# Loads of float64 weight pieces moved ahead of stores, kvb filled by two masked copies, wo1 spread over more steps

## The chip, the cores and the metric

The kernel runs on one core of a Trainium2 chip. The metric is the device time of one execution in microseconds (us). A core has TensorE (matmul; PE, and PEld for the load of its stationary operand), VectorE (DVE), ScalarE (ACT), GpSimd (POOL) and SyncE (SP); in this kernel every DMA is issued from SP's queue.

## The reference

Three layers, one after the other. An attention with 32 learned memory slots, over 8 batches, 8 heads, 576 positions, head size 64:

```python
a = phi - np.max(phi, axis=2, keepdims=True)
a = np.exp(a)
a = a / (np.sum(a, axis=2, keepdims=True) + 1e-09)
k_m = np.einsum('bhsm,bhsd->bhmd', a, k)
v_m = np.einsum('bhsm,bhsd->bhmd', a, v)
scores = scale * np.matmul(q, k_m.transpose(0, 1, 3, 2))
...
return np.matmul(attn, v_m)          # attn = softmax(scores)
```

Its output, as 4608 tokens of 512, goes through `h = max(max(x @ w1, x @ w2), x @ w3)` with 768 columns and `h @ w_out`, and that result through `(sigmoid(x @ w_gate) * (x @ w_val)) @ w_out` with 1536 columns. The activations are float32; the seven weight matrices are float64 and are turned into float32 on the chip.

## The kernel before

Matmuls take their operands as two parts, a rounded one and the rest, and add three products (`PASSES`).

**Weights.** A float64 weight comes as pieces of 128x384 64-bit words. `w_fetch` loads one into a tile `raw` (three buffers); `w_f32` (L122 to L126) makes float32 of it with two ScalarE and three VectorE instructions, the last of which (L126) reads `raw` for the last time; `w_split` makes the two parts on ScalarE (L131) and another engine (L73). `w_want` puts the next piece on the list `wq`, `w_have` takes the oldest from it, converts it, and for the first pass stores the split piece to `wxs`, from where later passes read it. `w_step` does a `w_have` and then the next `w_want`; `w_fill` fills `wq` up to three. `wx` (24 pieces) and `wo1` (8 pieces) go this way. The 48 pieces `wb` of the last layer go through `b_want` and `b_step`: convert the oldest, store it to `wbf`, load the next; `b_start` loads two ahead.

**Attention.** A group n is four heads of one batch; there are 16. `a0` takes the softmax of phi, with the reciprocal sums in `rs`; `a1` transposes it; `a2` multiplies it with k and v (L207) and copies the result, scaled by `rs`, into `kvb`: head s has partitions 32s to 32s+31, and goes into half `s % 2` of the columns, the other half staying at zero, so that the transposes of L227 in `a3` give block matrices. `kvb` is one of two tiles, filled with zeros once at the start. `a4` and `a5` make the second softmax.

**The passes.** The first part of the kernel is four passes of two batches each, `p`, of NS + NX = 24 + 16 steps `s`: `g_step` (v_m times wx, L342), `h_step` (the first layer, L369), then from step 24 on `x2_step` (times wo1, L392), one block d of 128 output columns in four steps. Block d reads pieces 2d and 2d+1 of wo1. Attention groups of the next pass are spread over the steps. `at(pos, fn)` hangs a weight step behind step `int(pos)`. The last layer follows (L687, L754).

**Order.** The instructions of an engine don't run in the program's order: the tile framework plans each engine's order in a timeline of its own, takes what is ready there, and prefers what stands earlier in the program. A load can go as soon as its tile's buffer is free. Two things bind the SP queue further: until `queue["in order"] = False`, every DMA stays in program order; and in the first pass `later` keeps the loads of phi, kv and q behind the last weight load traced so far.

Of the kernel before, what the change touches and what calls it, by code (L numbers as in the profile page):

```python
# [8 lines left out]
F32 = mybir.dt.float32  # L9
# [3 lines left out]
AF = mybir.ActivationFunctionType  # L13
ALU = mybir.AluOpType
AX = mybir.AxisListType
# [3 lines left out]
def attn_moe_kernel(  # L19
# [28 lines left out]
    vec, act, pool, pe, sync = nc.vector, nc.scalar, nc.gpsimd, nc.tensor, nc.sync  # L48
# [3 lines left out]
    def dma(o, i):  # L52
        ins = sync.dma_start(o, i)
        if queue["in order"]:
            tc.keep_in_program_order(ins)
        return ins
# [6 lines left out]
    def f32(ap):  # L63
        return ap.bitcast(F32)
# [16 lines left out]
    const = ctx.enter_context(tc.tile_pool(name="const", bufs=1))  # L81
    ident = const.tile([128, 128], F32, name="ident")
# [5 lines left out]
    att = tc.alloc_tile_pool(name="att", bufs=1, side="right")  # L88
    psA = tc.alloc_tile_pool(name="psA", bufs=8, space=PSUM)

    def bank():
        return psA.tile([128, 512], F32, tag="ps", name="ps")
# [12 lines left out]
    def w_fetch(pl, src):  # L105
        if not is64:
            w = pl.tile([128, PC], F32, tag="wf", name="wf", bufs=3)
            queue["last weights"] = dma(w, src)
            return w
        raw = pl.tile([128, PC], I64, tag="raw", name="raw", bufs=3)  # L110
        queue["last weights"] = dma(raw, src)
        return raw
# [17 lines left out]
    def w_split(w, hi, lo, eng=None):  # L130
        act.copy(hi, w)  # L131
        sub(eng or pool, lo, w, f32(hi))
# [35 lines left out]
        A[n]["q"].append(t)  # L168


    KVB = []
    for i in range(2):
        t = att.tile([128, 2, 2, 64], F32, name=f"kvb{i}")
        pool.memset(t, 0.0)
        KVB.append(t)

    def a0(n):
        st = A[n]
        nm = att.tile([128, 1], F32, tag="nm", name="nm", bufs=4)
        vec.tensor_reduce(out=nm, in_=st["phi"], axis=AX.X, op=ALU.max, negate=True)  # L180
        ss = att.tile([128, 1], F32, tag="ss", name="ss", bufs=4)
        et = st["et"] = att.tile([128, S], F32, tag="et", name="et", bufs=2)
        act.activation(out=et, in_=st["phi"], func=AF.Exp, bias=nm, accum_out=ss)
        rs = st["rs"] = att.tile([128, 1], F32, tag="rs", name="rs", bufs=4)
        vec.tensor_scalar(out=rs, in0=ss, scalar1=EPS, scalar2=None, op0=ALU.add)
        vec.reciprocal(out=rs, in_=rs)
        yield

    def a1(n):
# [10 lines left out]
    def a2(n):  # L200
        st = A[n]
        p = bank()
        es = st["es"]
        for c in range(5):
            r = 128 if c < 4 else 64
            for s in range(4):
                pe.matmul(  # L207
                    p[32 * s:32 * s + 32, :128],
                    lhsT=es[:r, c, 32 * s:32 * s + 32],
                    rhs=st["kv"][c][:r, 128 * s:128 * s + 128],  # L210
                    start=(c == 0), stop=(c == 4),
                )
        yield
        kvb = st["kvb"] = KVB[n % 2]
        for s in range(4):
            r = slice(32 * s, 32 * s + 32)
            act.activation(out=kvb[r, :, s % 2], in_=p[r, :128].rearrange("p (x d) -> p x d", x=2),
                           func=AF.Copy, scale=st["rs"][r])

    VT = {}  # L220

# [69 lines left out]
    wq = []  # L291

    def w_want(j, hp, p):
        if p == 0:
            wq.append((j, hp, p, w_fetch(mid, wx[j, hp] if j >= 0 else wo1[hp])))
        else:
            t = mid.tile([128, 2, PC], F32R, tag="wx", name="wx", bufs=6)
            dma(f32(t), wxs[j, hp])
            wq.append((j, hp, p, t))

    def w_have():
        j, hp, p, w = wq.pop(0)
        if j < 0:
            w = w_f32(mid, w)
            r = slice(hp * PC, hp * PC + PC)
            w_split(w, wo1_t[:, 0, r], wo1_t[:, 1, r])
            return
        if p == 0:
            w = w_f32(mid, w)
            t = mid.tile([128, 2, PC], F32R, tag="wx", name="wx", bufs=6)  # L310
            w_split(w, t[:, 0], t[:, 1])
            dma(wxs[j, hp], f32(t))
            w = t
        WX[j, hp] = w
# [4 lines left out]
    def b_want():  # L319
        if bplan:  # L320
            i, n = bplan.pop(0)
            bq.append((i, n, w_fetch(mid, wb[i, n])))

    def b_step():
        if not bq:
            return
        i, n, w = bq.pop(0)
        dma(wbf[i, :, n * PC:n * PC + PC], w_f32(mid, w))
        b_want()

    G = {}
    PASSES = ((1, 0), (0, 1), (0, 0))
# [201 lines left out]
    plan = []  # L534

    def w_step():
        if not wq:
            return
        w_have()
        if plan:  # L540
            w_want(*plan.pop(0))

    def w_fill():
        while plan and len(wq) < 3:
            w_want(*plan.pop(0))

    for t in range(len(stages) + 5):
# [37 lines left out]
    for p in range(NP):  # L585
        last = p == NP - 1
        side = {}

        def at(pos, fn, *a):
            side.setdefault(min(int(pos), NS + NX - 1), []).append((fn, a))  # L590

        if last:
            att.release()
            br = tc.alloc_tile_pool(name="br", bufs=1, side="right", reuse_waits="tile")
            at(NS, x_load, 0)
            at(NS, tw_load, 0)
            at(NS + 1, x_sums, 0, 0)
            at(NS + 2, x_sums, 0, 1)
            at(NS + 2, t_make, 0, ORDER[0])
            for n, pr in enumerate(ORDER):  # L600
                at(NS + 3 + n * 0.8, x_split, 0, pr, vec if n % 2 else None)
                if n:
                    at(NS + 8 + n * 0.8, t_make, 0, pr)
            at(NS + 14, wo_make, 0)
        for j in range(2, J):
            for hp in range(4):
                at(4 * (j - 2) + hp, w_step)
        if p == 0:
            def wo1_begin():
                plan.extend((-1, n, 0) for n in range(J * DM // PC))  # L610
                w_fill()
            at(4 * (J - 2) - 3, wo1_begin)
            for n in range(J * DM // PC):
                at(22 + n / 2, w_step)
        if not last:
            def w1_begin(p=p):
                plan.extend((j, hp, p + 1) for j in range(J) for hp in range(4))
                w_fill()
            at(29, w1_begin)
            for n in range(8):  # L620
                at(30 + n, w_step)
        if p == 0:
            for k in (0, 2, 4):
                at(3 + k // 2, later, load_ahead, k, 3)
        if p:
            n_b = 22 if last else 13
            end = NS - 1 if last else NS + NX
            at(0, b_start)
            for n in range(n_b):
                at(n * end / n_b, b_step)  # L630
        a_at, a_st = (0, 1.3) if p else (10, 1.1)
        atts = {}
        if not last:
            q = [(k, n) for n in range(4 * p + 4, 4 * p + 8) for k in range(len(stages))]
            for i, x in enumerate(q):
                atts.setdefault(min(int(a_at + i * a_st), NS + NX - 1), []).append(x)
            for n in range(4 * p + 4, 4 * p + 8):
                at(max(NS, a_at + a_st * (6 * (n - 4 * p) - 18)), a_split, n)
        for s in range(NS + NX):
            if last and s == NS:  # L640
                mid.release()
                b1 = tc.alloc_tile_pool(name="b1", bufs=1, side="right", reuse_waits="tile")
            gens = []
            for k, n in atts.get(s, ()):
                if len(atts[s]) > 1:
                    run(stages[k](n))
                    load_ahead(k, n)
                else:
                    gens.append(stages[k](n))
            if s < NS:  # L650
                j, u = divmod(s, 4)
                if j + 1 < J:
                    gens.append(g_step(p, j + 1, u))
                gens.append(h_step(p, j, u))
            else:
                d, u = divmod(s - NS, 4)
                if not last and 32 <= s < 36:
                    gens.append(g_step(p + 1, 0, s - 32))
                gens.append(x2_step(p, u, d))
            run(*gens)  # L660
            if len(atts.get(s, ())) == 1:
                if p == 0:
                    later(load_ahead, *atts[s][0])
                else:
                    load_ahead(*atts[s][0])
            for fn, a in side.get(s, ()):
                fn(*a)
# [201 lines left out]
```

## Time and profile before

| | us |
|---|---|
| median of 3 runs | 1414.42 |
| lowest and highest of them | 1409.95, 1415.02 |
| the profiled execution, its own time | 1413.25 |
| its span in the trace | 1411.5 |

| engine | busy us | share of the span |
|---|---|---|
| PE | 1353.1 | 96% |
| PEld | 1191.1 | 84% |
| DVE | 875.0 | 62% |
| ACT | 583.3 | 41% |
| POOL | 517.7 | 37% |

The time of an execution is that of the run; the span is what the trace covers of it, and lies 1.75 us below. Busy shares are means over stages that differ. A wait is listed with the engine that waits, the line, and what released it. A matmul's duration overlaps with its neighbours', so a number of matmuls in a stretch says more than their single durations.

### The profile page before, as it was taken

How to read it: one execution, taken by the hardware profiler on the slowest of the kernel's cores; microseconds unless marked ns; L12 is line 12 of the kernel's file. 1: busy time of each engine (PE TensorE's matmuls, PEld its weight loads, DVE VectorE, ACT ScalarE, POOL GpSimd, SP SyncE). 2: the span in 40 equal slices, each digit the busy share in tenths (PEclk: the TensorE clock that was granted, in tenths of full speed). 3: DMA queues.
4: the chain of work that ended last, by engine and by line, in shares of the span. 5: the costliest groups of instructions: out<-in, count | busy, mean ns of one | idle time of the engine just before them, and what ended most of it. 6: DMA issues, size and time to landing. Idle time of an engine off the chain costs nothing.

```text
span 1411.5 us, 22167 instructions
## 1 busy us (share of the span) xinstructions
PE 1353.1 (96%) x7864; PEld 1191.1 (84%) x7864; DVE 875.0 (62%) x1532; ACT 583.3 (41%) x1236; POOL 517.7 (37%) x456
## 2 busy tenths in 40 slices
PE   6588899989999999999999999999999999999998
PEld 3478798879999999878888888888888899999997
DVE  5989989987773575667765344454454534554454
ACT  6768667754653353353333221232222322133221
POOL 2666422241233126554487111371112712161211
PEclk8779999999999999999999999999999999999999
DMA  9588799878552433775546554465454666566651
GB/s 316 192 260 278 257 328 321 291 249 276 185 162 92 159 95 119 281 265 213 204 175 228 167 179 161 160 198 194 149 168 175 209 219 229 188 230 225 223 202 67
DMA packets 112269, 292.43 MB, mean 207 GB/s; under 512 B 12576, under 2 KB 28960, under 8 KB 112160
## 3 DMA queue, kind: packets, MB, share of 16 engines
q1 hardware_dynamic: 112160, 291.03, 60.8%
q8 instruction: 62, 1.02, 0.3%
q14 instruction: 47, 0.39, 0.1%
HBM read 224.92 MB, written 66.06 MB: 206 GB/s over the span
## 4 chain that ended last, share of the span: by engine, by line
PE 80%; DVE 7%; DMA 5%; issue 3%; ACT 3%; POOL 1%; SPq 0%; DVEq 0%; POOLq 0%; ACTq 0%
PE po L754 21%; PE px L687 15%; PE ps L369 11%; PE pz L687 10%; PE pv L687 10%; PE ps L392 8%; PE ps L342 3%; DMA raw<-wb_dram 1%; DVE ca L124 1%; DVE g L73 1%; PE ps L245 1%; DVE ca L126 1%; ACT g L356 1%; PE ps L207 1%; DMA q<-qT_dram 1%
## 5 line engine op out<-in xcount | busy, mean ns | idle before, releaser
L754 PE MATMUL po<-wo,gg 128*128 128x512 f32 x1296 | 332.8, 395 | 1.0 <-POOL gg L73 1.0
L73 POOL TENSOR_TENSOR gg<-gf,gg 128x512 fp32r<-128x512 f32 (+1 forms) x120 | 143.5, 1196 | 478.1 <-ACT gg L720 478.1
L754 PEld LDWEIGHTS po<-wo,gg 128*128 128x128 f32 x1296 | 242.5, 188 | 55.2 <-POOL gg L73 1.5
L369 PE MATMUL ps<-attn,g 128*128 128x288 f32 x1728 | 258.3, 304 | 18.3 <-POOL s L73 5.6
L369 PEld LDWEIGHTS ps<-attn,g 128*128 128x128 f32 x1728 | 247.5, 195 | 26.1 <-POOL s L73 5.9
L687 PE MATMUL px<-xa,tb 128*128 128x512 f32 (+1 forms) x1080 | 245.3, 369 | 1.6 <-ACT sg L710 1.3
L766 DVE TENSOR_TENSOR acc<-po,acc 128x512 f32<-128x512 f32 x180 | 124.3, 691 | 182.7 <-PE po L754 182.2
L687 PEld LDWEIGHTS px<-xa,tb 128*128 128x128 f32 x1080 | 198.1, 188 | 31.6 <-POOL tb L73 1.7
L687 PE MATMUL pz<-xa,tb 128*128 128x512 f32 (+1 forms) x720 | 171.0, 370 | 0.4 <-DVE x L70 0.4
L687 PE MATMUL pv<-xa,tb 128*128 128x512 f32 (+1 forms) x720 | 170.6, 369 | 0.0
L392 PE MATMUL ps<-h,wo 128*128 128x288 f32 x1152 | 161.4, 299 | 0.0
L392 PEld LDWEIGHTS ps<-h,wo 128*128 128x128 f32 x1152 | 157.3, 192 | 2.2 <-issue 1.9
L73 POOL TENSOR_TENSOR h<-hm,h 128x288 fp32r<-128x288 f32 x96 | 82.9, 865 | 196.7 <-ACT h L68 102.8
L687 PEld LDWEIGHTS pz<-xa,tb 128*128 128x128 f32 x720 | 132.2, 188 | 20.7 <-DVE x L70 0.8
L687 PEld LDWEIGHTS pv<-xa,tb 128*128 128x128 f32 x720 | 131.8, 188 | 18.9
L720 ACT CAST gg<-gf 128x512 fp32r<-128x512 f32 (+1 forms) x120 | 69.4, 579 | 179.6 <-DVE gf L716 132.7
L738 DVE TENSOR_TENSOR u<-pz,p 128x512 f32<-128x512 f32 (+1 forms) x120 | 76.2, 635 | 95.3 <-PE pz L687 89.2
L73 DVE TENSOR_TENSOR g<-ps,g 64x384 fp32r<-64x384 f32 x180 | 99.3, 552 | 32.7 <-ACT g L356 29.3
L356 ACT CAST g<-ps 64x384 fp32r<-64x384 f32 x192 | 90.7, 474 | 56.4 <-PE ps L342 30.4
L710 ACT ACTIVATE sg<-sg 128x512 f32<-128x512 f32 (+1 forms) x90 | 53.1, 590 | 146.8 <-DVE sg L708 146.6
L73 POOL TENSOR_TENSOR xa<-xf,xa 128x512 fp32r<-128x512 f32 (+1 forms) x64 | 78.7, 1252 | 19.9 <-ACT xa L131 19.9
L342 PE MATMUL ps<-wx,vt 128*128 128x384 f32 x288 | 73.0, 365 | 7.3 <-DVE g L73 3.0
(91 smaller groups left out, 1415.6 us busy)
## 6 DMA issues: line engine op xcount, KB each, us to landing
tb<-tbs SPq DMA_DIRECT2D x168, 512.0 KB, 3.7
wx<-wxs SPq DMA_DIRECT2D x72, 384.0 KB, 4.1
wo<-wos SPq DMA_DIRECT2D x48, 512.0 KB, 5.1
tbs<-tb SPq DMA_DIRECT2D x42, 512.0 KB, 2.9
raw<-wb_dram SPq DMA_DIRECT2D x48, 384.0 KB, 4.8
kv<-kvm_dram SPq DMA_DIRECT2D x48, 256.0 KB, 5.2
raw<-wx_dram SPq DMA_DIRECT2D x24, 384.0 KB, 4.0
wxs<-wx SPq DMA_DIRECT2D x24, 384.0 KB, 5.0
```

Source lines behind the costliest of these rows:

```text
L73: eng.tensor_tensor(out=o, in0=a, in1=b, op=ALU.subtract)
L124: vec.tensor_scalar(out=ai, in0=ai, scalar1=3, scalar2=None, op0=ALU.logical_shift_left)
L342: pe.matmul(ps[:, :384], lhsT=vt[:, x, 2 * e:2 * e + 2].rearrange("p a m -> p (a m)"), rhs=w[:, y], start=(n == 0), stop=(n == 2),)
L356: act.copy(t[r, 0], ps[r, :384])
L369: pe.matmul(ps[w][:, :U], lhsT=G[b, j, g][:, x, 128 * w:128 * w + 128], rhs=at[:, y, hf * U:hf * U + U], start=(n == 0), stop=(n == 5),)
L392: pe.matmul(ps[:, :U], lhsT=wo1_t[:, x, (d * J + j) * 128:(d * J + j) * 128 + 128], rhs=H[u, j][:, y], start=(n == 0), stop=(n == 3 * J - 1),)
L687: pe.matmul(ps[:, :half], lhsT=w[:, a, o:o + 128], rhs=x[:, k, c, :half], start=(first and n == 0), stop=(n == 5), skip_group_check=not first,
L710: act.activation(out=sg, in_=src, func=AF.Sigmoid)
L720: act.copy(t[:, 0, :half], gf)
L738: vec.tensor_tensor(out=u, in0=ps[:, :half], in1=E["p1", v], op=ALU.add)
L754: pe.matmul(ps, lhsT=GG[sc, j, c, h][:, x, 128 * m:128 * m + 128], rhs=WO[sc, j, h][:, y], start=(n == 0), stop=(n == 5),)
L766: vec.tensor_tensor(out=t, in0=ps, in1=t, op=ALU.add)
```

## The change

`b_step` and `w_step` issue the load of the next piece before they take, convert and store the piece in hand; `w_fill` fills to two. `kvb` becomes a tile that is written whole for each group: two copies over all 128 partitions, one for each half of the columns, with a scale `rm` that is `rs` where the head belongs to that half and zero elsewhere. `rm` is the product of `rs` and `mask`, which is summed once from the identity matrix. The eight steps of wo1, before behind the steps 22, 22, 23, 23, 24, 24, 25, 25, stand behind 22, 22, 24, 25, 27, 28, 29, 29.

```diff
@@ -168,11 +168,8 @@
         A[n]["q"].append(t)
 
 
-    KVB = []
-    for i in range(2):
-        t = att.tile([128, 2, 2, 64], F32, name=f"kvb{i}")
-        pool.memset(t, 0.0)
-        KVB.append(t)
+    mask = const.tile([128, 2], F32, name="mask")
+    vec.tensor_reduce(out=mask, in_=ident.rearrange("p (a s m) -> p s a m", s=2, m=32), axis=AX.XY, op=ALU.add)
 
     def a0(n):
         st = A[n]
@@ -184,6 +181,8 @@
         rs = st["rs"] = att.tile([128, 1], F32, tag="rs", name="rs", bufs=4)
         vec.tensor_scalar(out=rs, in0=ss, scalar1=EPS, scalar2=None, op0=ALU.add)
         vec.reciprocal(out=rs, in_=rs)
+        rm = st["rm"] = att.tile([128, 2], F32, tag="rm", name="rm", bufs=4)
+        vec.tensor_scalar(out=rm, in0=mask, scalar1=rs, scalar2=None, op0=ALU.mult)
         yield
 
     def a1(n):
@@ -211,11 +210,10 @@
                     start=(c == 0), stop=(c == 4),
                 )
         yield
-        kvb = st["kvb"] = KVB[n % 2]
-        for s in range(4):
-            r = slice(32 * s, 32 * s + 32)
-            act.activation(out=kvb[r, :, s % 2], in_=p[r, :128].rearrange("p (x d) -> p x d", x=2),
-                           func=AF.Copy, scale=st["rs"][r])
+        kvb = st["kvb"] = att.tile([128, 2, 2, 64], F32, tag="kvb", name="kvb", bufs=2)
+        for e in range(2):
+            act.activation(out=kvb[:, :, e], in_=p[:, :128].rearrange("p (x d) -> p x d", x=2),
+                           func=AF.Copy, scale=st["rm"][:, e:e + 1])
 
     VT = {}
 
@@ -324,9 +322,9 @@
     def b_step():
         if not bq:
             return
+        b_want()
         i, n, w = bq.pop(0)
         dma(wbf[i, :, n * PC:n * PC + PC], w_f32(mid, w))
-        b_want()
 
     G = {}
     PASSES = ((1, 0), (0, 1), (0, 0))
@@ -536,12 +534,12 @@
     def w_step():
         if not wq:
             return
-        w_have()
         if plan:
             w_want(*plan.pop(0))
+        w_have()
 
     def w_fill():
-        while plan and len(wq) < 3:
+        while plan and len(wq) < 2:
             w_want(*plan.pop(0))
 
     for t in range(len(stages) + 5):
@@ -611,7 +609,7 @@
                 w_fill()
             at(4 * (J - 2) - 3, wo1_begin)
             for n in range(J * DM // PC):
-                at(22 + n / 2, w_step)
+                at((22, 22, 24, 25, 27, 28, 29, 29)[n], w_step)
         if not last:
             def w1_begin(p=p):
                 plan.extend((j, hp, p + 1) for j in range(J) for hp in range(4))
```

## Rows read from the trace of the kernel before

**Rows 1.** Busy us (and instructions) of each engine in two stretches, clock, DMA.
```profile
48.00:350.00 302.00, 268.95 (x2023) 249.69 (x2023) 273.10 (x555) 203.03 (x476) 123.63 (x113) 0.92 0.82 278
...
583.00:1411.00 828.00, 822.05 (x3798) 699.36 (x3798) 427.32 (x636) 242.11 (x436) 288.02 (x238) 1.00 0.56 194
```

**Rows 2.** What matmuls waited for, 48 to 350 us: total, times, longest.
```profile
PE ps L227 <- ACT kvb L217: 8.3, 3, 5.5
```

**Rows 3.** Timeline, 306 to 318 us: start, us, engine, what [idle before].
```profile
306.42 0.53 DVE L126 SCALAR_TENSOR_TENSOR ca<-raw,ca 128x384 uint32<-128x384 uint32 x1
...
306.98 0.33 SPq L53 DMA_DIRECT2D wbf<-ca  x1
...
307.40 0.38 SPq L53 DMA_DIRECT2D raw<-wb_dram  x1
...
311.10 0.55 ACT L122 ACTIVATE ca<-raw 128x384 f32<-128x384 f32 x1 [1.59 <-DMA raw<-wb_dram]
...
311.99 1.46 ACT L217 ACTIVATE kvb<-ps,rs 32x128 f32<-32x128 f32 x4
...
313.50 0.69 PE L227 MATMUL ps<-ident,kvb 128*128 128x128 f32 x2 [5.52 <-ACT kvb L217]
...
313.84 4.09 PE L392 MATMUL ps<-h,wo 128*128 128x288 f32 x18
```

**Rows 4.** Timeline, 167 to 174 us.
```profile
167.05 0.55 ACT L122 ACTIVATE ca<-raw 128x384 f32<-128x384 f32 x1 [1.17 <-DMA raw<-wb_dram]
...
169.45 0.44 PE L227 MATMUL ps<-ident,kvb 128*128 128x128 f32 x2 [2.26 <-ACT kvb L217]
...
169.64 4.10 PE L392 MATMUL ps<-h,wo 128*128 128x288 f32 x18
```

**Rows 5.** Chain that ended last, in order of time: start, us, what.
```profile
319.06 9.72 PE ps L392 x72
```

**Rows 6.** What ScalarE waited for, 150 to 350 us: total, times, longest.
```profile
ACT ca L122 <- DMA raw<-wb_dram: 23.6, 22, 3.0
```

**Rows 7.** The DMA queue (SP) in order of time, 148 to 159 us.
```profile
148.52 0.33 SPq L53 DMA_DIRECT2D raw<-wb_dram  x1
...
153.41 0.33 SPq L53 DMA_DIRECT2D raw<-wb_dram  x1
```

**Rows 8.** The same queue, 158 to 194 us.
```profile
158.58 0.33 SPq L53 DMA_DIRECT2D raw<-wb_dram  x1
162.86 0.33 SPq L53 DMA_DIRECT2D wbf<-ca  x1
...
192.38 1.44 SPq L53 DMA_DIRECT2D wbf<-ca  x2
193.88 0.50 SPq L53 DMA_DIRECT2D raw<-wb_dram  x1
```

**Rows 9.** Groups by line and shape, whole run: busy us, mean ns | idle before.
```profile
L217 ACT ACTIVATE kvb<-ps,rs 32x128 f32<-32x128 f32 x64 | 23.0, 359 | 4.6 <-PE ps L207 3.7
...
L271 DVE TENSOR_SCALAR sm<-sm 128x18 f32<-128x18 f32 x16 | 5.2, 324 | 0.1
...
L230 ACT COPY kt<-ps 128x128 f32<-128x128 f32 x16 | 4.2, 264 | 2.9 <-PE ps L227 2.8
...
L185 DVE TENSOR_SCALAR rs<-ss 128x1 f32<-128x1 f32 x16 | 2.3, 141 | 4.3 <-ACT et L183 4.3
```

**Rows 10.** Timeline, first 5 us: first work of VectorE.
```profile
3.71 0.75 DVE L180 TENSOR_REDUCE nm<-phi 128x1 f32<-128x576 f32 x1 [3.71 <-DMA phi<-phiT_dram]
```

**Rows 11.** The DMA queue (SP), first pass, 83 to 85 us.
```profile
83.90 0.38 SPq L53 DMA_DIRECT2D raw<-wx_dram  x1
84.33 0.45 SPq L53 DMA_DIRECT2D phi<-phiT_dram  x1
```

**Rows 12.** Work on tile wo, 100 to 240 us: ns min/median/max, first and last start.
```profile
L392 PE MATMUL ps<-h,wo x288: 290/295/442, 160.0 to 211.6; 128*128 128x288 f32 x144
L131 ACT CAST wo<-ca x8: 512/512/515, 122.3 to 158.5; 128x384 fp32r<-128x384 f32 x8
```

## The prediction

> **What bounds the kernel now.** I read the busy time by stretches first, since the share over the whole span mixes stages. In the second half TensorE is busy 822 of 828 us at the full clock of 2.4 GHz [rows 1]; nothing that this change touches runs there, and nothing is to be had there. From 48 to 350 us it is another picture: TensorE is busy 269 of 302 us, at a granted clock of 0.92, while VectorE is busy 273 us and ScalarE 203 us. So about 33 us of idle TensorE, and the time at the lower level of 1.2 GHz that follows idle stretches, are all that a change in the front can win. The conversion of the float64 weights fills VectorE's gaps in it.
>
> Next, the list of waits of the matmul queue in this stretch: the largest entry is the transposes of L227, which wait 8.3 us in three stops for the copies to kvb in L217 [rows 2]. The timeline shows what the two large ones are made of. At 308 us TensorE stands 5.52 us before L227, because ScalarE has a conversion of L122 ahead of L217 in its queue and waits 1.59 us for that one's raw piece, until 311.10 us; then come the four copies, 1.46 us [rows 3]. At 167 us it is the same picture, smaller: 1.17 us for a raw piece, then the copies, 2.26 us of idle TensorE [rows 4]. After each, a group of 18 matmuls of L392 takes 4.09 or 4.10 us [rows 3, 4], where 72 of them take 9.72 us later, 2.43 us for 18 [rows 5]: the clock fell behind the stop, for another 1.67 us each time. In all ScalarE waits 23.6 us, 22 times, for raw pieces of wb between 150 and 350 us [rows 6]; most of it stops no matmul.
>
> **The change, part by part.** First, the load ahead of the store. In the program, b_step issues the store of piece n, then the load of piece n+2; afterwards the load comes first. If the SP queue followed the program, the load would have stood behind a store that waits for the conversion. But the queue of before shows three loads of wb, at 148.52, 153.41 [rows 7] and 158.58 us, ahead of the first store at 162.86 us [rows 8]. The planner already takes the third load ahead. What holds a load is its buffer: the last conversion step of an older piece ends at 306.42 + 0.53 = 306.95 us, its store goes at 306.98 and the load into the freed buffer at 307.40 us [rows 3]. That store is three pieces older than the load, so it is ahead of it in both programs. I went through the 48 loads of wb so: 36 go within 1.5 us after their buffer is free. Only where two stores go together, as at 192.38 us with the load at 193.88 [rows 8], can the new order help, by about one store's 0.3 to 1.4 us of issue. Cost and gain: 0, with a bound of 23.6 us of ScalarE's waits from above [rows 6] if the loads do come earlier, and of 1.5 us of SP issue from below.
>
> For w_step the same holds more plainly: with two filled instead of three and the load first in each step, the loads and stores come in the same sequence as before (L2, S0, L3, S1, ...), with the same three buffers. Only the place in the program moves by a step. That place matters in one spot: loads of phi, kv and q in the first pass are queued behind the last weight load traced so far, as phi at 84.33 us right behind the weight piece at 83.90 [rows 11]. They may now go one weight piece, some 4 us, sooner. The list of [rows 2] has no wait for a DMA in it, so I count 0; if they delay a weight piece, it is by their own issue, 0.45 us for one.
>
> Second, the copies. Four ScalarE copies of 32 partitions become two of 128. The elements in a partition stay 128, and a copy of 128 by 128 without scale takes 264 ns where one of 32 by 128 with a scale takes 359 ns [rows 9]: the time is not set by the partitions. I take 359 ns each (bounds 264 and, if nothing is saved by halving their number, 2 x 359). A group of heads saves 2 x 0.36 = 0.72 us on ScalarE, 16 groups 11.5 us, 8 groups in the stretch 5.7 us. On the path it counts where L227 waits: in the two large stops 0.72 us each, in the small third one (8.3 - 5.52 - 2.26 = 0.5 us) 0.5 us: together 1.9 us. Elsewhere ScalarE's shorter queue is covered by VectorE's.
>
> What it adds: 16 products rm of 128x2 on VectorE. The rows around are 141 ns for 128x1 and 324 ns for 128x18 [rows 9]; 128x2 is nearer to the first, so 0.14 us. Eight in the stretch make 1.1 us (2.6 us at 324 ns; 0 where VectorE is idle, and it is busy 90% of the stretch [rows 1]): I count 1.0 us. Its place in the queue is ahead of the other groups' reductions, and the copies now wait for rm, 0.14 us behind rs, two stages before they are due. The mask is one reduction of 128x128 at the start, under the 0.75 us that a reduction of 128x576 takes, and VectorE does nothing until 3.71 us, when phi lands [rows 10]; it costs 0 there, and up to 0.75 us if that cover were gone. Two fills of kvb on GpSimd go, ahead of anything that waits.
>
> Third, wo1. Its eight pieces were cast between 122.3 and 158.5 us, the first matmul that reads them starts at 160.0 us and the last of the pass at 211.6 us [rows 12]. They run as fast as buffers come free, long before the steps that the program names, so a later step changes only who goes first among ready work. The second pair of pieces is needed only after the first four groups of 18 matmuls. I count 0; the gain is bounded by the two stops, the loss is the last rival below.
>
> Sum: 1413.25 - 1.9 + 1.0 = 1412.35, say 1412 us. The profiled execution's 1413.25 us stands 1.2 us under the median of the three runs shown, 1414.42. A measurement of this kernel tells about 0.5% from no change, so below 1407.3 is faster and above 1421.5 slower.
>
> **The rivals.** *The stops go.* If the new sequence (loads that do come earlier, or merely another order of ScalarE's queue) takes L217 out from behind waiting conversions, both stops vanish with their clocks: 5.52 + 2.26 + 2 x 1.67 = 11.1 us, 1402 us. For it: both have the one form, and the change shortens or moves two of its three parts. Against: the loads are held by buffers, which the change leaves at three.
>
> *VectorE sets the pace.* It is the fullest engine beside TensorE in the stretch. Then ScalarE's saving is worth nothing and the 16 products cost their whole time, 1.1 to 2.6 us in the stretch: 1415 us, no measurable change either. The Trainium skill says as much (Perfetto Trace Analysis, Identifying the Most-Contended Engine): improve the engine with the highest occupancy first. By that rule the halved copies give nothing, and the trace speaks against it. By the rows alone: VectorE still has 29 us idle in the stretch [rows 1], and TensorE stops 8.3 us for ScalarE's copies [rows 2], so this case gets the smallest chance.
>
> *wo1 comes late.* If the planner does follow the later steps, x2_step of the first pass reaches its second block before pieces 2 and 3 are split, and TensorE stops. Pieces were cast every (158.5 - 122.3) / 7 = 5.2 us [rows 12]; two that are still out cost 10.4 us, and the clock behind the stop 1.67 us: 1425 us. It decides from the second missing piece; one alone gives 1420. Against it: every piece was cast before the first of them was read.
>
> **How the numbers follow.** Forecast, 1412 us: 0.38. VectorE's pace, 1415 us: 0.10. The stops go, 1402 us: 0.33. wo1 late, 1425 us: 0.19. So faster 0.33, the same 0.48, slower 0.19. The forecast's own range is 1409 to 1418: 1.9 us of saving or none, 2.6 us of rm, and the runs' spread of 2.5 us to either side. The range given goes 4 us below the rival at 1402, an eighth of the 33 us of idle TensorE that a new order could take along, to 1398, and up to a single late piece, 1420; two late pieces, 0.19, lie outside.
>
> **What would show it.** Right: the group of L217 with 32 instead of 64 at about 0.36 us; loads of raw still within 1 us after a conversion ends; three loads of wb ahead of the first store; the 583 to 1411 us part unchanged; TensorE idle about 32 us in the front. Wrong: stops before L227 gone or longer than 5 us, a shorter list of ScalarE's waits for raw, matmuls of L392 that wait for wo1, or casts of wo1 after 160 us. Since each engine's order is planned anew, the weakest step is that the two stops stay where they are.

## The result, and the profile after

The changed kernel takes 1394.26 us (median of four runs, 1389.95 to 1395.26) against 1414.29 us for the kernel before: ratio 0.9859, interval 0.9830 to 0.9888. It is 20 us faster. The forecast was 1412 us, and the time lies below the range of 1398 to 1420. The profiled execution took 1393.47 us, with a span of 1391.6 us.

The first look is again at the busy time by stretches, here of the kernel after, for the stretches of [rows 1] (the last one ends 20 us sooner):

```profile
48.00:350.00 302.00, 274.58 (x2128) 254.15 (x2129) 277.45 (x578) 200.47 (x475) 125.83 (x115) 0.95 0.84 280
...
583.00:1391.00 808.00, 803.94 (x3766) 692.74 (x3764) 419.68 (x628) 238.53 (x432) 285.30 (x236) 1.00 0.58 196
```

The front gets 105 more matmuls done in the same 302 us (2128 for 2023). The surprise is the second row. In [rows 1] 3798 matmuls took 822.05 us of busy time, 216.4 ns each; now 3766 take 803.94 us, 213.5 ns each, at the same full clock and with no instruction of that part changed. Two windows of 100 us inside the last layer, 600 to 700 and 700 to 800 us, say it without durations. First before, then after:

```profile
600.00:700.00 100.00, 99.77 (x433) 80.65 (x432) 68.92 (x89) 43.64 (x75) 48.23 (x36) 1.00 0.60 220
700.00:800.00 100.00, 100.00 (x435) 81.26 (x434) 56.15 (x76) 34.06 (x58) 60.74 (x46) 1.00 0.60 210
```

```profile
600.00:700.00 100.00, 100.00 (x441) 82.55 (x440) 67.36 (x90) 39.74 (x68) 48.23 (x37) 1.00 0.56 206
700.00:800.00 100.00, 100.00 (x441) 82.55 (x440) 51.37 (x71) 35.62 (x61) 55.22 (x43) 1.00 0.59 202
```

TensorE is full in all four rows, yet it gets through 441 matmuls instead of 433 and 435. So the 20 us fall into two parts that can be read from one matmul's start in each trace. The first matmul of the last layer (L687, after L685) starts at 578.43 us before and at 567.78 us after: 10.65 us come from the front. Its row in TensorE's timeline, 565 to 585 us, before and after:

```profile
578.43 2.92 PE L687 MATMUL px<-xa,tb 128*128 128x512 f32 x12
```

```profile
567.78 1.56 PE L685 MATMUL px<-xa,tb 128*128 128x512 f32 x6
```

The last one of the up products, that is the products of L687 (L685), starts at 1397.77 and 1378.08 us: 9.04 us more come from the last layer, at an even rate. The products of L754 (L752), which read gg, are the down products.

In the front the waits of TensorE's matmul queue, 48 to 350 us, have changed places. The stop of 5.52 us at 308 us [rows 3] is gone, and of the 8.3 us of [rows 2] 2.5 us are left; the largest entry is now another:

```profile
PE ps L367 <- DVE g L73: 12.4, 4, 8.1
...
PE ps L225 <- ACT kvb L215: 2.5, 2, 2.1
```

ScalarE's waits for raw pieces, 150 to 350 us, have grown from the 23.6 us of [rows 6]:

```profile
ACT ca L122 <- DMA raw<-wb_dram: 32.5, 20, 4.3
```

The two groups that the change brought, whole run, against [rows 9]:

```profile
L215 ACT ACTIVATE kvb<-ps,rm 128x128 f32<-128x128 f32 x32 | 9.9, 361 | 7.8 <-PE ps L206 7.6
L185 DVE TENSOR_SCALAR rm<-mask,rs 128x2 f32<-128x2 f32 x16 | 5.4, 336 | 0.2
```

One thing must be known for the experiments: kernels whose engines run the same instructions in the same order still differ by some us in the front of a single trace. Six such kernels below, with only unused bytes added, start their last layer between 0.94 us sooner and 3.69 us later than before. A shift of under 4 us in one trace proves nothing; the medians and the last layer's rate do.

### The profile page after: what moved, and what is told of

Same layout as the page of the kernel before. It is cut to its first block, busy times and chain, and to the rows that moved or that the text cites. A ratio compares the mean times of both kernels' runs of the same rounds, so it can differ in the third digit from the quotient of the medians.

```text
span 1391.6 us, 22154 instructions
## 1 busy us (share of the span) xinstructions
PE 1335.2 (96%) x7864; PEld 1184.2 (85%) x7864; DVE 872.3 (63%) x1549; ACT 567.8 (41%) x1204; POOL 519.3 (37%) x454
## 4 chain that ended last, share of the span: by engine, by line
PE 80%; DVE 9%; DMA 5%; issue 3%; ACT 1%; POOL 1%; SPq 0%; DVEq 0%; ACTq 0%
PE po L752 21%; PE px L685 16%; PE ps L367 11%; PE pz L685 11%; PE pv L685 10%; PE ps L390 6%; PE ps L340 2%; DVE ca L126 2%; DVE g L73 1%; DVE ca L124 1%; DMA raw<-wb_dram 1%; DVE ca L125 1%; PE ps L206 1%; PE ps L243 1%; DVE hm L378 1%
## 5 line engine op out<-in xcount | busy, mean ns | idle before, releaser
L752 PE MATMUL po<-wo,gg 128*128 128x512 f32 x1296 | 327.7, 392 | 1.0 <-POOL gg L73 1.0
L752 PEld LDWEIGHTS po<-wo,gg 128*128 128x128 f32 x1296 | 242.4, 188 | 49.5 <-POOL gg L73 1.3
L367 PE MATMUL ps<-attn,g 128*128 128x288 f32 x1728 | 254.6, 301 | 19.4 <-DVE g L73 12.4
L367 PEld LDWEIGHTS ps<-attn,g 128*128 128x128 f32 x1728 | 244.2, 193 | 26.9 <-issue 14.0
L685 PE MATMUL px<-xa,tb 128*128 128x512 f32 (+1 forms) x1080 | 244.0, 368 | 3.2 <-DVE x L70 3.2
L685 PEld LDWEIGHTS px<-xa,tb 128*128 128x128 f32 x1080 | 198.1, 188 | 31.5 <-DVE x L70 3.6
L685 PE MATMUL pv<-xa,tb 128*128 128x512 f32 (+1 forms) x720 | 169.2, 367 | 0.0
L685 PE MATMUL pz<-xa,tb 128*128 128x512 f32 (+1 forms) x720 | 169.1, 367 | 0.0
L390 PE MATMUL ps<-h,wo 128*128 128x288 f32 x1152 | 158.4, 296 | 0.6 <-DVE hm L379 0.6
L685 PEld LDWEIGHTS pz<-xa,tb 128*128 128x128 f32 x720 | 132.1, 188 | 18.6
L685 PEld LDWEIGHTS pv<-xa,tb 128*128 128x128 f32 x720 | 131.9, 188 | 17.7
L714 DVE TENSOR_TENSOR gf<-gf,sg 128x512 f32<-128x512 f32 (+1 forms) x90 | 71.5, 795 | 9.5 <-ACT sg L708 1.3
```

The source lines that it names most:

```text
L367: pe.matmul(ps[w][:, :U], lhsT=G[b, j, g][:, x, 128 * w:128 * w + 128], rhs=at[:, y, hf * U:hf * U + U], start=(n == 0), stop=(n == 5),)
L390: pe.matmul(ps[:, :U], lhsT=wo1_t[:, x, (d * J + j) * 128:(d * J + j) * 128 + 128], rhs=H[u, j][:, y], start=(n == 0), stop=(n == 3 * J - 1),)
L685: pe.matmul(ps[:, :half], lhsT=w[:, a, o:o + 128], rhs=x[:, k, c, :half], start=(first and n == 0), stop=(n == 5), skip_group_check=not first,
L714: vec.tensor_tensor(out=gf, in0=gf, in1=sg, op=ALU.mult)
L752: pe.matmul(ps, lhsT=GG[sc, j, c, h][:, x, 128 * m:128 * m + 128], rhs=WO[sc, j, h][:, y], start=(n == 0), stop=(n == 5),)
```

## The experiments

All ratios are to the kernel before on the same chip. "The 109th matmul of H" in the expectations is the 109th of L369 (the first layer); it starts at 86.62 us before and 76.57 us after. A "conversion" is one weight piece through L124 to L126 on VectorE. Where an order is told, it is that of the compiled program.

**The last layer: unused bytes.** The mask takes 8 bytes of each partition in a pool that lies below the others, and in the program's memory plan everything on the left side then begins 32 bytes higher: gg at 36512 instead of 36480. First, the kernel before with as much unused memory (e1), and the changed kernel with its mask on the right side, where it moves nothing of the last layer (e2):

```diff
+    spare = const.tile([128, 2], F32, name="spare")
+    pool.memset(spare, 0.0)
```

> The kernel before with one unused tile of 8 bytes a partition beside the identity, filled once on GpSimd at the start. It takes the place that mask takes after, so every tile of the pools low and mid, and of the last layer's pool on the same side, lies 32 bytes higher, as in the changed kernel; the order of the instructions stays that of before. Theory A (the 32 bytes give the faster pace of the last layer, 8.5 us of the 20): 1405.7 us, the stretch from the first matmul of L687 to the end about 8.5 us shorter, the front as before. Rival B (the pace comes from the new order or from how one execution fell): 1414 us, no difference.

Measured: 1404.31 us, ratio 0.9936 (0.9924 to 0.9949). The last layer starts at 578.50 us, as before, and its last up product 9.66 us sooner.

```diff
-    mask = const.tile([128, 2], F32, name="mask")
+    mask = att.tile([128, 2], F32, name="mask")
```

> The changed kernel with mask in the pool of the attention tiles, on the other side of the memory: the same order of instructions as the changed kernel, but the tiles of the last layer at the addresses of before. Theory A (32 bytes): the last layer at the pace of before, 1394.3 + 8.5 = 1402.8 us. Rival B (order or execution): 1394 us. In both the first matmul of the last layer at about 568 us, if the front's gain has nothing to do with addresses.

Measured: 1401.88 us, ratio 0.9919 (0.9905 to 0.9932); down products at 395 ns, as before. So 8 bytes that no instruction of the last layer touches are worth 7.6 us (e2 against the changed kernel) to 9.5 us (e1). Which tile, and is it the shift or the place? Four more, all with the order of TensorE, VectorE, ScalarE and SP of before. Everything on the left 64 bytes higher (e8):

> Kernel before plus an unused tile of 64 bytes for each partition, so that the left side's tiles lie 64 bytes higher; the order of TensorE, VectorE, ScalarE and SP is that of before. In before gg begins at 36480, a multiple of 64, and xa and wo2 at 32 above a multiple of 64; with 32 bytes more gg stands as they do. Theory 'place within 64 bytes': no gain, 1412 to 1417, mean of the down matmuls 395 ns. Theory 'any other place' (any shift does it): 1403 to 1407 and 392 ns. In between or slower would say that it goes by larger steps.

Only gg, u7 and acc 32 bytes higher (e10):

```diff
+        if "spare" not in E:
+            E["spare"] = b2.tile([128, 8], F32, name="spare")
+            pool.memset(E["spare"], 0.0)
         t = GG[sc, j, c, h] = b2.tile([128, 2, 512], F32R, tag="gg", name="gg", bufs=6)
```

> Kernel before plus an unused tile of 32 bytes for each partition in the last layer's pool, just ahead of gg: gg, u7 and acc lie 32 bytes higher, tw, p1, u6, sg and gf and everything of the first layer lie as before; the order of TensorE, VectorE, ScalarE and SP is that of before. Theory 'gg' (TensorE's stationary operand of the down matmuls, or acc and u7 beside it): the whole 8 to 9.5 us of the last layer come, 1404 to 1407, down mean 392 ns. Theory 'scratch tiles' (sg, gf, p1, u6): nothing, 1412 to 1416, 395 ns.

p1, u6, sg and gf 32 bytes higher, gg, u7 and acc 64 (e11):

> Kernel before plus 32 bytes ahead of p1 and 32 bytes ahead of gg: p1, u6, sg and gf lie 32 bytes higher, gg, u7 and acc 64 bytes higher, tw and the first layer as before; same order of engines. Theory 'gg': nothing, 1412 to 1416, since a shift of everything by 64 bytes gave 395 ns. Theory 'scratch tiles': the 8 to 9.5 us, 1404 to 1407, 392 ns. If both this and the run with gg alone give a part, each share adds up to 8 to 9.5 us.

Only u7 and acc 32 bytes higher (e14):

> Kernel before with 32 unused bytes between gg and u7: u7 and acc lie 32 bytes higher, gg as before. Theory 'gg': nothing, 1411 to 1416, down mean 395 ns. Theory 'acc or u7': 1403 to 1406, 392 ns.

Measured: 1412.71 us (0.9985, 0.9972 to 0.9999), 1404.41 us (0.9928, 0.9913 to 0.9943), 1412.15 us (0.9987, 0.9975 to 0.9998) and 1413.15 us (0.9997, 0.9985 to 1.0009). Only the one that puts gg itself at 32 above a multiple of 64 gains 9 us; the other three stay within 2 us of the kernel before. The groups of the down products (po) and one of the up products (pv), whole run, of the kernels with 64 bytes, with gg alone, and with u7 and acc alone:

```profile
L756 PE MATMUL po<-wo,gg 128*128 128x512 f32 x1296 | 332.6, 395 | 1.0 <-POOL gg L73 1.0
...
L689 PE MATMUL pv<-xa,tb 128*128 128x512 f32 (+1 forms) x720 | 170.2, 368 | 0.0
```

```profile
L757 PE MATMUL po<-wo,gg 128*128 128x512 f32 x1296 | 327.8, 392 | 1.0 <-POOL gg L73 1.0
...
L687 PE MATMUL pv<-xa,tb 128*128 128x512 f32 (+1 forms) x720 | 169.3, 367 | 0.0
```

```profile
L757 PE MATMUL po<-wo,gg 128*128 128x512 f32 x1296 | 332.9, 395 | 1.0 <-POOL gg L73 1.0
...
L687 PE MATMUL pv<-xa,tb 128*128 128x512 f32 (+1 forms) x720 | 170.7, 369 | 0.0
```

In before xa already begins at 32 above a multiple of 64. The last of this set moves xa down by 32 bytes, to a multiple of 64, and leaves gg (e15):

> Kernel before with 32 unused bytes on the right side: xa and xf lie 32 bytes lower, xa then begins at a multiple of 64 as gg does; gg, wo2 and tb as before. Theory 'gg against xa' (the two must have the same place within 64 bytes): 1403 to 1406, down mean 392 ns. Theory 'gg's own address': nothing, 1411 to 1416, 395 ns; slower if an operand at a multiple of 64 costs wherever it stands.

Measured: 1417.04 us, ratio 1.0025 (1.0015 to 1.0036): slower. The same two groups:

```profile
L756 PE MATMUL po<-wo,gg 128*128 128x512 f32 x1296 | 332.4, 395 | 1.0 <-POOL gg L73 1.0
...
L689 PE MATMUL pv<-xa,tb 128*128 128x512 f32 (+1 forms) x720 | 171.9, 371 | 0.0
```

The down products stay at 395 ns and the up products, which read xa, go from 369 to 371 ns in the mean of both their shapes. So it is not gg's place against xa's. Two theories are left. One is that an operand of TensorE at a multiple of 64 bytes costs, whichever of the two it is; the kernel before has one such operand in its last layer, gg. The other is that the two operands of one product must have the same place within 64 bytes: in the memory plan wo2, which the down products read with gg, and tb, which the up products read with xa, begin at 32 above a multiple of 64 in all these kernels. Every slow pair here has one operand at a multiple of 64 and the other 32 above one, every fast pair has both 32 above one, and no kernel has both at a multiple of 64 in this layer. Which of the two it is stays open, and so does why the chip does it.

Nor does the whole gain sit where gg is read. From before to e10 the busy time of the down products falls by 5.0 us (332.8 to 327.8 us), and that of the three groups of up products by 4.1 us together, though xa and tb are not moved. That gg's place slows its neighbours too is what the runs show; how, they don't.

**The front: the copies.** The masked copies alone, with the mask on the right side and loads and wo1 as before (e3):

> The kernel before with the masked copies alone (mask, rm, two copies of 128 partitions; mask on the side of the attention tiles, so that the addresses of before hold). Theory C (the copies and the order that comes with them give the front's 10.6 us): 1403.7 us, the first matmul of the last layer near 568 us. Rival D (the moved loads give them): 1412 us, 578 us, that is my sum of the prediction.

Measured: 1401.35 us, ratio 0.9914 (0.9901 to 0.9928), the last layer at 568.17 us. The masked copies, priced at a net 0.9 us, give 12 us. But not where the prediction looked for it: the largest stop before the transposes is still there, 5.0 us (this kernel's waits of the matmul queue, 48 to 350 us):

```profile
PE ps L367 <- DVE g L73: 13.2, 6, 8.1
PE ps L225 <- ACT kvb L215: 5.0, 1, 5.0
```

Ten of the 12 us are there by 77 us already. Counted from the trace's start to the 109th matmul of H, VectorE has done this in before (first 86.6 us) and in this kernel (first 76.6 us):

```profile
L369 PE MATMUL ps<-attn,g 128*128 128x288 f32 x108 | 22.0, 366 | 11.3 <-POOL s L73 5.6 <-ACT hf L379 3.1 <-ACT g L356 1.4
L125 DVE CUSTOM_DVE_ANT_0 ca<-ca,cr 128x768 uint16<-128x768 uint16 x17 | 14.0, 830 | 0.3
L126 DVE SCALAR_TENSOR_TENSOR ca<-raw,ca 128x384 uint32<-128x384 uint32 x17 | 12.7, 752 | 0.1
L124 DVE TENSOR_SCALAR ca<-ca 128x384 uint32<-128x384 uint32 x17 | 12.7, 750 | 3.0 <-ACT ca L122 3.0
```

```profile
L367 PE MATMUL ps<-attn,g 128*128 128x288 f32 x108 | 20.3, 349 | 11.8 <-DVE g L73 8.1 <-DVE hm L379 1.5 <-ACT attn L281 1.2
...
L126 DVE SCALAR_TENSOR_TENSOR ca<-raw,ca 128x384 uint32<-128x384 uint32 x14 | 11.6, 829 | 0.2
```

and in the stretch from 48 to 100 us, in before and in this kernel:

```profile
48.00:100.00 52.00, 37.01 (x191) 33.42 (x192) 48.60 (x87) 37.08 (x83) 34.02 (x32) 0.76 0.71 235
```

```profile
48.00:100.00 52.00, 43.20 (x290) 40.84 (x294) 51.25 (x94) 40.39 (x92) 35.56 (x33) 0.88 0.68 236
```

The same 108 matmuls, but 14 conversions ahead of them instead of 17. One takes 0.75 + 0.83 + 0.75 = 2.33 us on VectorE, which is nearly full there (48.60 and 51.25 of 52 us); three are 7.0 us. The granted clock is 0.88 for 0.76, and the idle TensorE straight ahead of the 108 matmuls is about the same (11.3 and 11.8 us). So the theory: with other instructions in the list, the planner put three conversions behind the work that TensorE waits for. The 7.0 us are an estimate from these rows and leave 3 us of the early gain unaccounted for. The rival: ScalarE's shorter copies. Two kernels tell them apart. One keeps the four copies and computes rm beside them, unused (e5):

> Kernel before plus the mask and the product rm on VectorE (20 of them), with the four old copies kept; rm is computed and not used. The mask lies where it shifts no tile of the last layer. ScalarE saves nothing. In the order of VectorE's instructions 17 weight pieces are converted ahead of the tenth hm, as in before (14 in the kernel with the masked copies alone). Theory 'deferred conversions' (the 10 us of the masked copies are gained between 50 and 87 us because three conversions of about 2.4 us are put behind the work that TensorE waits for): the 109th matmul of H stays at 86 to 88 us, the median is 1412 to 1417. Theory 'ScalarE's time' says the same here. Theory 'any new order' (the 10 us come with whatever new plan): gains or losses of several us by 90 us.

Measured: 1408.06 us, ratio 0.9955 (0.9939 to 0.9971), with 17 conversions ahead and the 109th matmul at 88.14 us. The front expected is right, the time is 4 us under what both theories gave: a new order with only more work in it is worth 6.5 us by itself, half of what the masked copies gave, with no conversion put behind. The other makes each masked copy twice (e6):

```diff
-        for e in range(2):
+        for e in (0, 1, 0, 1):
```

> The masked copies alone, but each of the two is made twice, so that ScalarE makes four copies for each item as before, over all 128 partitions. Its own order of VectorE has 15 conversions ahead of the tenth hm and 16 ahead of the twelfth (before 17 and 17, masked copies alone 14 and 15). Theory 'deferred conversions': the gain between 50 and 87 us stays, the 109th matmul of H comes at 77 to 80 us, the median at 1401 to 1406. Theory 'ScalarE's time' (the two copies saved are what the path gained): the gain goes, the 109th matmul of H comes at 85 to 88 us, the median at 1411 to 1416.

Measured: 1406.48 us, ratio 0.9933 (0.9908 to 0.9958), the 109th matmul at 77.77 us with 14 conversions ahead, the last layer 7.30 us sooner than before. ScalarE makes as many copies as before and 8.85 of the 9.94 us of the early gain are there. That leaves some 3 us, from 10.25 to 7.30 us, that its saving could have given; but this is within the scatter of single traces, the intervals of the two ratios overlap, and the order is not quite that of e3, so no run shows that the saving gives anything.

Then the order alone, without masked copies. The conversion of a piece is queued on VectorE behind the hm (the last max of h_step) of the step in which it is traced (e9):

```diff
+        hms.append(vec.tensor_tensor(out=m, in0=ps[2][:, :U], in1=m, op=ALU.max))
...
+                        with tc.issue_after(hms[-1].ins):
+                            w_step()
```

> Kernel before with its four copies, its mask-free memory and its loads; one thing is added: in the first pass a weight piece's conversion on VectorE is queued behind the hm of the step it is traced in (issue order alone). VectorE's order then has 14 conversions ahead of the sixth hm, 15 ahead of the tenth and 16 ahead of the twelfth (before 15, 17, 17; masked copies alone 13, 14, 15; masked copies made twice 13, 15, 16). Theory 'deferred conversions': about two of the three conversions are out of the way, so the 109th matmul of H comes at 78 to 83 us and the median falls to 1403 to 1410. Theory 'the masked copies themselves': nothing is gained there, 85 to 88 us and 1411 to 1416.

Measured: 1412.68 us, ratio 0.9991 (0.9981 to 1.0001). One conversion only was put back by the 109th matmul (16 ahead), which came 2.05 us sooner; the last layer began 1.94 us later than before. Too little, and lost again. With the step one later the order has as many conversions ahead as with the masked copies (e13):

```diff
-                at(4 * (j - 2) + hp, w_step)
+                at(4 * (j - 2) + hp + (1 if p == 0 else 0), step)
```

> Kernel before with its four copies; in the first pass a weight piece's conversion is traced one step later and queued on VectorE behind the hm of that step. VectorE's order has 13 conversions ahead of the sixth hm, 14 ahead of the tenth, 15 ahead of the twelfth: the numbers of the masked copies alone (before 15, 17, 17). Theory 'deferred conversions': the 109th matmul of H at 76 to 79 us, first matmul of the last layer at 567 to 574 us, median 1402 to 1409. Theory 'the masked copies themselves': the 109th at 84 us or later, median 1410 to 1416.

Measured: 1401.54 us, ratio 0.9908 (0.9886 to 0.9930): the gain of the masked copies, with the four old copies kept. The way there is another one: the 109th matmul comes at 81.92 us, later than expected, the difference is 9.95 us at 305 us, and the stop before the transposes, 5.52 us in [rows 3], is 1.73 us here (TensorE's timeline, 290 to 312 us):

```profile
299.80 0.44 PE L227 MATMUL ps<-ident,kvb 128*128 128x128 f32 x2 [1.73 <-ACT kvb L217]
```

One, two and three steps, each with the 32 bytes at gg (e16 to e18):

> The two causes together with no part of the change: the conversions queued back as in the run with the same order, and gg, u7 and acc 32 bytes higher. Theory 'both causes': the time of that run less 8 to 9.5 us, 1393 to 1400, near the changed kernel's 1394.3. If either cause is only a by-product of the masked copies: 1402 or more.

> As the run with both causes, but a weight piece's conversion is traced two steps later and queued behind the hm of that step: 12 conversions ahead of the sixth hm, 13 ahead of the tenth, 14 ahead of the twelfth, 19 ahead of the 24th (with one step 13, 14, 15, 20). Theory 'each conversion put back is worth its 2.4 us until a weight piece is late': 1388 to 1392. Theory 'one lucky order': any time between 1392 and 1405.

> The same with three steps: 12 conversions ahead of the sixth hm, 13 ahead of the tenth, 13 ahead of the twelfth, 20 ahead of the 24th. Theory 'each conversion put back is worth its 2.4 us until a weight piece is late': 1386 to 1392, or slower than one step with a wait of TensorE for a wx piece in the trace. Theory 'one lucky order': any time between 1392 and 1405.

Measured: 1392.32 us (0.9847, 0.9826 to 0.9868), 1394.42 us (0.9855, 0.9827 to 0.9882) and 1399.40 us (0.9882, 0.9845 to 0.9919). The first has the change's whole gain and none of its parts; its 1392.32 us, the best of all, is within the spread of the changed kernel's runs. Putting back more does not go on paying: with three steps some 5 us of the gain are lost again. So it is an order that is worth 12 us. That the conversions ahead are the larger part of it is not shown. Counted in the compiled order, e13 and e16 have as few of them ahead as e3; yet at the 109th matmul e13 is 4.70 us sooner than before and e16, in the same order as e13, 2.15 us, where e3 is 9.94 us sooner. Both win the rest later, and start the last layer 14.06 and 13.40 us sooner. The 2.33 us a conversion describe e3's trace; they are no rule.

**The front: the loads.** Both halves (e4), then w_step's alone (e12):

> The kernel before with the moved loads alone (b_step, w_step, w_fill to two); kvb, wo1 and all addresses as before. Rival D (the loads give the front's 10.6 us): 1403.7 us, first matmul of the last layer near 568 us. Theory C (the copies do): 1414 us and 578 us; a load is held by its buffer and not by the store.

> Kernel before with the w_step half of the loads' part alone (the next piece wanted before the one in hand is converted, w_fill to two); b_step as before. Theory 'w_step carries it' (the two halves together gained 5.6 us between 87 and 113 us, in the first pass, where b_step does not run): 217th matmul of H at 107 to 109 us, 1406 to 1411. Theory 'b_step carries it': 112 to 114 us, 1412 to 1416.

Measured: 1408.23 us, ratio 0.9967 (0.9955 to 0.9979), and 1410.88 us, ratio 0.9966 (0.9954 to 0.9979). So w_step's half carries it. The load of phi goes one weight piece sooner than in [rows 11] (SP's queue of the kernel with w_step's half alone):

```profile
79.80 0.33 SPq L53 DMA_DIRECT2D raw<-wx_dram  x1
80.19 0.71 SPq L53 DMA_DIRECT2D phi<-phiT_dram  x1
```

and the two windows behind it, 85 to 100 and 100 to 115 us, hold 229 matmuls instead of 195. First before, then this kernel:

```profile
85.00:100.00 15.00, 12.12 (x78) 10.96 (x77) 14.75 (x29) 12.07 (x29) 11.40 (x11) 0.96 0.94 287
100.00:115.00 15.00, 14.45 (x117) 13.65 (x115) 13.42 (x27) 10.43 (x25) 6.85 (x7) 0.82 0.92 296
```

```profile
85.00:100.00 15.00, 14.69 (x99) 14.23 (x99) 14.26 (x31) 13.02 (x31) 11.66 (x12) 0.95 0.94 333
100.00:115.00 15.00, 14.17 (x130) 12.99 (x128) 13.56 (x32) 13.71 (x35) 9.15 (x10) 1.00 0.77 254
```

In this kernel, the one with both halves and e9, the first product of the last layer waits 4.4 to 4.5 us for a VectorE copy of the pass before it (3.2 us in the changed kernel), which gives back that much: in the kernel with both halves the gain was 8.56 us until then and 3.90 us behind it.

**What adds up.** The masked copies with the mask where the changed kernel has it, loads and wo1 as before (e7):

> The masked copies alone with the mask where the changed kernel has it, so that the tiles on the left side lie 32 bytes higher; the loads and wo1 as in before. The order of every engine is that of the masked copies alone. Theory 'two causes that add' (deferred conversions in the front, 32 bytes in the last layer): 1401.4 less the 8 to 9.5 us of the last layer, 1391 to 1394, which is the changed kernel's time without its two other parts. If the loads and wo1 add something of their own on top of these: 1396 or more.

Measured: 1393.38 us, ratio 0.9841 (0.9822 to 0.9861), as fast as the whole change. On top of the masked copies the loads and wo1 give nothing that can be told. The wo1 steps alone were not run: that kernel compiles to the same instructions in the same order on every engine as before.

## Why the prediction was wrong, point by point

**"Nothing that this change touches runs there"** (583 to 1411 us) is the step that failed first. The sum and the range put the last layer at nothing, and it holds 9.04 of the 20 us. The instructions are untouched; their operand gg is not, because mask moved it by 32 bytes. e1, e2 and e10 show it: 9.1 to 9.5 us from unused bytes, none when the mask lies elsewhere. The second step that failed is that the front keeps its order: there the sum had a net 0.9 us, and 10.65 us were gained.

**The copies: right price, wrong account.** A masked copy takes 361 ns, as taken (359 ns). An rm takes 336 ns in the mean, not 140; but twelve of the sixteen take 209 to 243 ns (median 228), and four long ones, 376 to 1030 ns, lift the mean. The mean of the 128x18 row, 324 ns, is lifted in the same way (median 172 ns). So 0.14 us was too low, and the two means agree by their long ones, not by their shapes. Sixteen cost 5.4 us of VectorE. But the net of -1.9 and +1.0 us was made for an order that stays. In e3 the stop at 308 us, from which 0.72 us should have come, is still 5.0 us, and nearly all of the gain, 9.94 of 10.25 us, is made before 87 us, in a place that the sum did not have. e6 leaves ScalarE's saving some 3 us of it, within the scatter of single traces; e13 makes as much without the copies.

**The loads: right mechanism, wrong value.** Of the 48 loads of wb 36 go within 1.5 us after their buffer is free, in both kernels, and moving b_step's showed nothing. That phi, kv and q "may now go one weight piece, some 4 us, sooner" is what happened, 84.33 to 80.19 us. The step valued it at 0 because no matmul's wait named a DMA; alone it is worth some 5 us (ratios 0.9967 and 0.9966 in e4 and e12). Whether it is phi's arrival or the new order that goes with it was not told apart.

**wo1: right in its price.** The rows of the tile, of the kernel after, 100 to 240 us:

```profile
L390 PE MATMUL ps<-h,wo x288: 288/294/442, 150.3 to 203.0; 128*128 128x288 f32 x144
L131 ACT CAST wo<-ca x8: 495/513/515, 126.7 to 160.1; 128x384 fp32r<-128x384 f32 x8
```

The last three of the eight casts now start behind the first reading matmul (150.6 to 160.1 us), and no matmul waits for one. So "casts of wo1 after 160 us" was a poor sign of being wrong: it came, and cost nothing.

**The rivals.** "The stops go" was in part what happened: in the changed kernel the copies stand ahead of the conversion that waits, and TensorE stands 0.47 us where it stood 5.52 us (timeline of the kernel after, 299 to 308 us):

```profile
302.83 0.63 ACT L215 ACTIVATE kvb<-ps,rm 128x128 f32<-128x128 f32 x2
...
303.51 0.44 PE L225 MATMUL ps<-ident,kvb 128*128 128x128 f32 x2 [0.47 <-ACT kvb L215]
305.91 0.55 ACT L122 ACTIVATE ca<-raw 128x384 f32<-128x384 f32 x1 [2.46 <-DMA raw<-wb_dram]
```

What that is worth shows in two places of the front. The first matmul of the second pass that reads wo1 starts here, before (TensorE's timeline, 297 to 300 us) and after (292 to 296 us):

```profile
298.33 1.87 PE L392 MATMUL ps<-h,wo 128*128 128x288 f32 x12
```

```profile
294.03 2.26 PE L390 MATMUL ps<-h,wo 128*128 128x288 f32 x15
```

Behind the stop come the 72 matmuls that [rows 5] have at 319.06 us; in the chain of the kernel after they are:

```profile
308.30 9.72 PE ps L390 x72
```

Of the 10.05 us that the 109th matmul of H came sooner, 4.30 us are left at the first place; at the second it is 10.76 us. So in this trace the larger part of the front's gain, 6.46 us, is won between the two, where the stop stood, while in e3 the stop stays and the front gains as much. That the rival's 11.1 us lie so near the front's 10.65 us is in part luck: its second stop is still there, 2.1 of 2.26 us. Its 1402 us was the nearest of the four times and still 8 us off, since the other half lay in the last layer. "VectorE sets the pace" got the smallest chance for the wrong reason: I read from VectorE's idle 29 us that it has room, and from 48 to 100 us it has little: 48.60 of 52 us are busy before. The Trainium skill's rule to improve the most occupied engine first (Perfetto Trace Analysis, Identifying the Most-Contended Engine) points there. This case agrees as far as e3 goes: its early gain falls where VectorE is 51.25 of 52 us busy, though the change lightened ScalarE; no run here made VectorE's work there less.

The prediction did call it the weakest step that the stops stay where they are, since every engine's order is planned anew; what it lacked was a price for that. The measured one, from kernels that change little else: no gain (e9), 6.5 us (e5) and 12 us (e13). Which part of a new order gives it stays open.

## What to carry to other kernels

Before an edit is priced at its own instructions, look at what else moves with it: the addresses of tiles allocated behind a new one, and the planned order of the whole kernel. A small unused tile and an unused instruction are cheap controls for both. Where an engine is full in a stretch, ask which of its work no one waits for yet, try to queue that behind the rest by hand, and measure more than one place: behind the same step it gave nothing here (e9), one step later 12 us (e13). And look at the rate of a part that "is not touched" in the profile after, before explaining a gain by what was touched.

## What the runs showed of the hardware

TensorE's products in the last layer take 0.5 to 0.9% longer when gg or xa begins at a multiple of 64 bytes in a partition than at 32 above one, while the other operand of the product stands at 32 above one: 395 against 392 ns for the down products with gg (e8, e10), 371 against 369 ns for the mean of pv with xa (e15, before). Durations overlap; by count it is 433 and 435 against 441 in 100 us. With gg moved, the up products beside it go faster as well, 369 to 367 ns. Whether the multiple of 64 counts or the unequal places of the two operands, no run here tells. The Trainium skill (SBUF — State Buffer, Operand start alignment) asks only for a multiple of the element's size and says that this is about legality, its runs timed nothing; here the place had a price of 9 us in 1414.
